# RWKV-7 scan and a cosine-gated expert layer on one core: the ways of x^T in chunks 1 to 3, and three instead of four conversion steps between two steps of chunk 1

## The chip, the cores and the metric

The kernel runs on one core of a Trainium2 chip. The metric is the device time of one execution in microseconds (us), lower being better. It is compared by medians of several executions. Engines are named as in the profile: PE is TensorE (matmuls), PEld its weight loads, DVE is VectorE, ACT is ScalarE, POOL is GpSimd, and SP is SyncE, whose queue issues nearly all DMAs of the stretch that this document is about.

## The reference

```python
# attention: r, k, v, w, a, b are (4, 8, 768, 40)
for t in range(S):
    y[:, :, t] = np.einsum('bhd,bhde->bhe', rt, state)
    Sa = np.einsum('bhde,bhe->bhd', state, at)
    state_decay = state * wt[:, :, None, :] - np.einsum('bhd,bhe->bhde', Sa, bt)
    state = state_decay + np.einsum('bhd,bhe->bhde', vt, kt)
# bridge: x is (3072, 320), one row per batch and position
h = x @ w_in            # 320 -> 2048
g = h * np.cos(h)
out = g @ w_out         # 2048 -> 320
```

The inputs of the attention are float32. `w_in` and `w_out` come as float64 and are used as float32, so the kernel reads their 64-bit words and makes float32 of them itself.

## The kernel before

The 768 positions go in 24 chunks of 32. Each chunk turns the recurrence into small matrix products and a triangular solve; only the state goes from one chunk to the next. Two chunks make a group of 256 tokens for the expert layer. The whole program's order is written out by hand: every engine works its instructions in the order in which the Python code records them, and waits where an operand isn't ready.

**One chunk.** `main(c)` gives five segments: `t` (`ch_t`, transposes the state `qz` into `s`), `q` (`ch_q`), `x` (`ch_x`, right sides; copied to `x0` by ACT and DVE), `s` (`ch_s`, the solve by the inverse `rt`; its result is copied and masked into `sm`), and `z` (`ch_z`, products `dps` that give the new state `qz` and the output `yt`). `p2(c + 1)` gives three segments that prepare the next chunk: `v`, `k` and `g` (`p2_g`, the products `gram`, masked into `ag` and `vvm`). Every four chunks need an inverse, made on DVE by `by_blocks` or `inverse`. For chunks 0 to 7 its lower half is made by TensorE instead, one chunk at a time: `pair_first` (`F1`, `F2`, ...) and `pair_second` (`S1`, `S2`, ...), whose sum goes into `rt` on DVE (L567). `p1(c)` gives `pw`, `pa`, `pb`, `pn`, which prepare decays and inverse for two chunks from 4 on; they hold the reciprocals L395.

**The way of x^T.** In `ch_z` DVE writes `yt` by four additions (L762), which alternate with four for the state (L755); POOL scales the state in four products (L756) and then multiplies `yt` by the decay (L767). Two segments later `tokens` stores `yt` to a buffer `xd` in HBM (L776), and one segment later `back` loads it as `xT` (L786, L788). Both go on SP, and the load waits for the store.

**Expert layer.** `pieces` is a list of short works: `first_a` and `first_b` make `ph = xT . w_in` for a quarter of the 2048 columns, followed by rounding, cosine and product (`turns`, L830 to L840, giving `gT`); `second` makes `po = gT . w_out`. In the lists of segments an `M` stands where the next piece goes. A group's pieces may run from the chunk after its second one.

**The weights' conversion.** The weights are cut into 20 blocks of 128x512. For each, `rounded` gives `fetch` (SP, L237), `taken` (DVE L245 and L246, ACT L249 and L251), `mantissa` (DVE L255, ACT L258) and `product` (DVE L261, then POOL L264 for the sign). `w_steps` lists them mixed: product of n, fetch of n + 3, mantissa of n + 1, taken of n + 2. `step(seg, of_inv, of_w)` records a segment, then what was put off with `later` and is due, then `of_inv` steps of the inverse and `of_w` of `w_steps`. The pair comes from `fill`: (1, 4) in chunk 1, (0, 2) in chunk 2, (2, 3) in chunk 3. `F` and `S` segments before chunk 3 pass (0, 0). `later(n, ...)` counts segments, so a segment more or less moves what is put off. What is left of `w_steps` is recorded before `pn4`.

**The scan of w.** `ws_scan` makes running products of the decays of four chunks at once, nine operations on DVE (L170 and L175). `scanned(q)` does it, puts off the store to HBM (`ws_store`, L180) by two segments and the fetch of the next four chunks (`ws_fetch`, L161) by twelve. `scanned(2)` stands in chunk 3.

**Idle fills.** `busy(n)` and `kept_busy(n)` record n matmuls on zeros that nothing reads. `busy` follows each segment of chunk 1, and those of chunk 2 until the first piece is done; `FILL` maps (chunk, place in the list) to a count for `kept_busy`.

**Buffers.** Most products go to the PSUM pool `at`, which has two buffers: a segment that takes one waits until the last but one user has been read. `ph` and `po` have pools of two buffers each.

Of the kernel before, what the change touches and what calls it, by code (L numbers as in the profile page):

```python
# [20 lines left out]
def kernel(  # L21
# [43 lines left out]
    nc = tc.nc  # L65
# [97 lines left out]
            bass.AP(w.tensor, w.offset + q * n, [[S * D, B * H], [C * D, 4], [1, C * D]]),  # L163
        )

    def ws_scan(q):
        n = 1
        while n < C:
            to = ws[:, 2 * n - 1 :: 2 * n]
            nc.vector.tensor_tensor(to, to, ws[:, n - 1 :: 2 * n], ALU.mult)  # L170
            n *= 2
        n = C // 4
        while n:
            to = ws[:, 3 * n - 1 :: 2 * n]
            nc.vector.tensor_tensor(to, to, ws[:, 2 * n - 1 : C - 1 : 2 * n], ALU.mult)  # L175
            n //= 2

    def ws_store(q):
        wd[q] = dram.tile([B, H, 4, C, D], F32, tag="wd", name="wd")
# [546 lines left out]
    def ch_z(c):  # L726
        ps = [at("dps") for _ in range(2)]
        sm = G["sm"]

        wide = c > 3  # L730
        for bb in range(0 if wide else B):
            for e in range(2):
                mm(
                    ps[bb // 2][full[e], bb % 2, : 4 * N72], idle[blk[bb], :DP],
                    pick(idle[blk[bb]], 0, (0, 4), (1, N72)), True,
                )
        for s, n in ((0, kn_b[c % 2]), (1, bn_b[c % 7])):
            for j in range(4):
                o = C - C * (j // 2)
                for bb in range(B):  # L740
                    for e in range(2):
                        first = wide and not s
                        mm(
                            ps[bb // 2][(full if first else half)[e], bb % 2, j * N72 : (j + 1) * N72],
                            n[blk[bb], 2 * j + e, : DP if first else D],
                            sm[e][blk[bb], j, :] if s else vvm[c % 2][blk[bb], 2 * j + e, o : o + N72],
                            first and j == 0,
                        )
        wx, wc = G["wx", c], G["wc", c]
        yt = sb1.tile([P, 4, B, C], F32, tag="yt", name="yt")  # L750
        for bb in range(B):
            dp = ps[bb // 2][:, bb % 2]
            if c < NCH - 1:
                z = pick(qz[:, bb], C, (DP, 2), (NZ, 2), (1, D))
                nc.vector.tensor_tensor(z, pick(dp, 0, (2 * N72 + C, 2), (N72, 2), (1, D)), z, ALU.add)  # L755
                nc.gpsimd.tensor_tensor(  # L756
                    z, z,
                    wc.rearrange("p (f m b) -> p f m b", f=2, m=2)[:, :, :, bb]
                    .unsqueeze(3).to_broadcast([P, 2, 2, D]),
                    ALU.mult,  # L760
                )
            nc.vector.tensor_tensor(  # L762
                yt.rearrange("p (f m) b t -> p f m b t", f=2)[:, :, :, bb],
                pick(dp, D, (2 * N72 - D, 2), (N72, 2), (1, C)),
                pick(qz[:, bb], 0, (NZ - C, 2), (NZ, 2), (1, C)), ALU.add,
            )
        nc.gpsimd.tensor_tensor(  # L767
            yt.rearrange("p j b t -> p (j b) t"), yt.rearrange("p j b t -> p (j b) t"), wx, ALU.mult
        )
        later(2, lambda: tokens(c, yt))  # L770
# [133 lines left out]

        return [first_w, both_a, lambda: p1_b(c), lambda: p1_n(c)]

    def scanned(q):

        ws_scan(q)
        later(2, lambda: ws_store(q))  # L910
        if q + 1 < NCH // 4:
            later(12, lambda: ws_fetch(q + 1))
# [17 lines left out]
    with tc.manual_schedule():  # L930
# [115 lines left out]
        firsts = [lambda n=n: pair_first(0, n, n > 2) for n in range(4)]  # L1046
        seconds = [lambda n=n: pair_second(0, n, n > 2) for n in range(4)]
        (F1, F2, F3), (S1, S2, S3) = firsts[1:], seconds[1:]
        FILL = {(1, 6): 6, (1, 9): 14, (2, 0): 6, (2, 3): 6, (2, 5): 4, (2, 11): 29, (3, 3): 13, (3, 4): 20}
        for c in range(NCH):  # L1050
            t, q, x, s, z = main(c)
            v, k, g = p2(c + 1) if c + 1 < NCH else [lambda: None] * 3
# [2 lines left out]
            if c == 0:  # L1055
                segs = []
            elif c == 1:
                segs, fill = [t, F1, v, q, k, S1, x, g, s, z], (1, 4)
            elif c == 2:
                for n, m, name in ((11, 5, "a"), (14, 4, "b")):  # L1060
                    later(n, lambda m=m, name=name: load(m, name))
                segs, fill = [t, F2, v, q, S2, k, M, x, M, F3, g, M, s, S3, M, z, M, M], (0, 2)
            elif c == 3:
                pw4, pa4, pb4, pn4 = p1(4)
                pw, pa, pb, pn = p1(6)
                segs = [
                    t, pw4, M, q, pa4, M, x, lambda: scanned(2), M, s, pw, M, pb4, pa, M, pn4, M, z, M,
                    pb, v, pn, k, M, g,
                ]
                for n, m, name in ((1, 5, "b"),):  # L1070
                    later(n, lambda m=m, name=name: load(m, name))
                fill = (2, 3)
            elif c == 4:
                pw, pa, *p8 = p1(8)
                firsts = [lambda n=n: pair_first(4, n) for n in range(4)]
                seconds = [lambda n=n: pair_second(4, n) for n in range(4)]
                F4, F5, F6, F7 = firsts
                S4, S5, S6, S7 = seconds
                segs = [
                    t, v, M, q, M, k, x, M, F4, M, S4, F5, M, s, F6, M, pw, F7, M, z, M, g, M, pa, S5, lambda: scanned(3),  # L1080
                ]
                fill = (2, 0)
            elif c == 5:
                pw, pa = p1(10)[:2]
                pb, pn = p8
                segs = [t, M, pb, q, M, pn, k, M, x, M, s, S6, M, z, M, S7, M, pw, v, M, g, pa, M]
            elif c % 4 == 0 and q0 < NCH:
                pb, pn = p1(q0)[2:]
                segs = [t, v, M, q, M, k, x, M, g, M, s, pb, M, z, M, pn, M, M]
                if q0 + 4 < NCH:  # L1090
                    segs.insert(-1, lambda: scanned(c // 4 + 2))
            elif c % 4 == 1 and q0 < NCH:
                pw, pa = p1(q0 + 2)[:2]
                segs = [t, M, pw, q, M, x, k, M, s, v, M, z, M, pa, M, g, M, M]
            elif c % 4 == 2 and q0 < NCH:
                pb, pn = p1(q0 + 2)[2:]
                segs = [t, M, pb, q, M, pn, v, M, x, M, s, k, M, g, M, z, M, M]
            elif c % 4 == 3 and q0 + 4 < NCH:
                pw, pa = p1(q0 + 4)[:2]
                segs = [t, M, pw, q, M, x, k, M, s, v, M, z, M, pa, M, g, M, M]  # L1100
            else:
                segs = [t, v, M, q, M, x, k, M, g, M, s, M, M, z, M, M]
# [10 lines left out]
            for i, seg in enumerate(segs):  # L1113
# [7 lines left out]
                    w_steps.pop(0)()  # L1121
                if seg is not M:
                    G["kind"] = "q" if seg is q and c > 3 else "other"
                    step(seg, *((0, 0) if c < 3 and seg in (*firsts, *seconds) else fill), small=seg in (q, x, g, s, z, pn, pn4, *firsts, *seconds))
                    if seg not in (*firsts, *seconds) and (c < 2 or c == 2 and not done):
                        busy({s: 6, q: 5, v: 4, k: 4, z: 4}.get(seg, 3))
                else:
# [45 lines left out]
```

## Time and profile before

| what | us |
| --- | --- |
| median of 3 runs | 802.15 |
| the runs | 800.43, 803.71, 802.15 |
| profiled execution | 800.58 |
| its span, first to last instruction | 798.9 |
| PE busy | 745.9 (93%) |
| PEld busy | 571.0 (71%) |
| DVE busy | 486.7 (61%) |
| ACT busy | 383.4 (48%) |
| POOL busy | 199.9 (25%) |
| last `yt` addition (L762) of chunks 0, 1, 2, 3, start | 61.97, 92.28, 126.08, 161.45 |
| product L767 of these chunks, start | 62.55, 94.11, 126.66, 162.09 |
| store `xd` issued | 64.30, 95.59, 127.95, 165.10 |
| load `xT` issued | 69.42, 97.87, 130.23, 170.00 |
| first operation of the scan in chunk 3, last one's end | 145.93, 149.87 |

The table's busy times are sums over the span. The idle fills count as busy time of PE, and so does the time in which matmuls queue in it. What one stretch is limited by is read from that stretch alone: from the busy time of each engine in a window cut at the chunks' borders, from the timeline, where an instruction carries the idle time before it and what ended that in brackets, and from the chain of waits.

### The profile page before, as it was taken

What the parts mean: (1) busy time and instruction counts of PE and PEld (TensorE: products, weight loads), DVE (VectorE), ACT (ScalarE), POOL (GpSimd) and SP (SyncE); (2) the same over time, 40 slices, a digit from 0 to 9 for tenths busy, and PEclk for the clock granted to TensorE, in tenths of its full rate; (3) what the DMA queues carried; (4) which work ended last, traced back from release to release, by engine and by line L of the source; (5) the groups of instructions that cost most, each with busy time, mean ns of one, the idle gap of its engine ahead of it and who ended that gap; (6) DMA issues with size and microseconds to landing.
All of it is one profiled execution on the core that took longest, in us unless ns stands there. A gap on an engine that the chain in (4) does not pass through costs nothing.

```text
span 798.9 us, 39602 instructions
## 1 busy us (share of the span) xinstructions
PE 745.9 (93%) x17812; PEld 571.0 (71%) x17812; DVE 486.7 (61%) x1025; ACT 383.4 (48%) x723; POOL 199.9 (25%) x354
## 2 busy tenths in 40 slices
PE   4768798999999999999999999999999999999997
PEld 4535576777766777777777787777787777777775
DVE  8768858864734896554895645994346863323331
ACT  1336567564435436545535635534545445354352
POOL 5326635230321330330330230332031122201000
PEclk9888899999999999999999999999999999999999
DMA  8575563343353314334214324223220222001000
GB/s 112 150 187 140 146 152 88 60 124 64 59 122 64 67 36 65 72 99 70 60 38 66 93 43 73 46 49 68 43 46 21 46 46 55 19 18 32 20 17 16
DMA packets 183304, 55.79 MB, mean 70 GB/s; under 512 B 157152, under 2 KB 178656, under 8 KB 183136
## 3 DMA queue, kind: packets, MB, share of 16 engines
q1 hardware_dynamic: 177440, 52.11, 30.6%
q8 instruction: 140, 2.29, 1.2%
q10 hardware_dynamic: 5440, 0.82, 0.8%
q0 software_dynamic: 256, 0.33, 0.3%
q14 instruction: 28, 0.23, 0.1%
HBM read 42.07 MB, written 11.14 MB: 67 GB/s over the span
## 4 chain that ended last, share of the span: by engine, by line
PE 65%; DVE 14%; DMA 5%; ACT 5%; issue 4%; POOL 3%; SPq 2%; DVEq 0%; ACTq 0%; POOLq 0%
PE ph L101 22%; PE po L101 20%; PE x0ps L101 3%; PE dps L101 3%; PE gram L101 3%; DVE rw L395 3%; PE vT L330 2%; PE sps L101 2%; PE qps L101 2%; PE nps L101 2%; DVE inv_tmp L494 2%; DVE inv L498 2%; DVE mant L245 1%; SPq L152 1%; PE kT L330 1%
## 5 line engine op out<-in xcount | busy, mean ns | idle before, releaser
L101 PE MATMUL po<-w_out_sb,gT 128*128 128x320 f32 x768 | 223.5, 439 | 0.1
L101 PE MATMUL ph<-xT,w_in_sb 128*128 128x256 f32 x768 | 185.7, 386 | 0.1
L101 PEld LDWEIGHTS po<-w_out_sb,gT 128*128 128x128 f32 x768 | 140.2, 190 | 54.6 <-issue 2.3
L101 PEld LDWEIGHTS ph<-xT,w_in_sb 128*128 128x128 f32 x768 | 139.3, 190 | 29.7 <-issue 12.4
L830 ACT ACTIVATE turns<-ph,rnd 128x512 f32<-128x512 f32 x96 | 64.1, 685 | 156.3 <-PE ph L101 155.9
L832 DVE SCALAR_TENSOR_TENSOR turns<-turns,ph 128x512 f32<-128x512 f32 x96 | 64.0, 683 | 109.4 <-ACT turns L830 109.2
L840 DVE TENSOR_TENSOR gT<-ph,turns 128x512 f32<-128x512 f32 x96 | 65.8, 686 | 38.4 <-ACT turns L837 38.4
L756 POOL TENSOR_TENSOR qz<-qz,wc 128x160 f32<-128x160 f32 x92 | 41.9, 475 | 168.5 <-DVE qz L755 167.9
L837 ACT ACTIVATE turns<-turns,half_pi 128x512 f32<-128x512 f32 x96 | 69.3, 722 | 3.1
L836 ACT ACTIVATE turns<-turns 128x512 f32<-128x512 f32 x96 | 60.1, 626 | 19.0 <-DVE turns L832 19.0
L101 PE MATMUL ph<-xT,w_in_tail 64*128 64x256 f32 (+1 forms) x512 | 54.6, 394 | 1.6 <-issue 1.6
L498 DVE TENSOR_TENSOR inv<-inv,inv_tmp 128x31 f32<-128x31 f32 (+15 forms) x124 | 51.2, 413 | 4.3
L755 DVE TENSOR_TENSOR qz<-dps,qz 128x160 f32<-128x160 f32 x92 | 28.9, 314 | 37.6 <-PE dps L101 37.3
L586 POOL COPY vp<-nat_v 128x320 f32<-128x320 f32 x24 | 11.7, 487 | 159.9 <-DMA nat_v<-in_v_dram 139.6
L494 DVE TENSOR_TENSOR inv_tmp<-u,inv 128x31 f32<-128x31 f32 (+15 forms) x124 | 48.5, 391 | 2.3
L395 DVE RECIPROCAL rw<-nat_w 128x320 f32<-128x320 f32 x20 | 42.8, 2142 | 0.1
L101 PEld LDWEIGHTS ph<-xT,w_in_tail 64*128 64x128 f32 (+1 forms) x512 | 32.2, 160 | 10.8 <-issue 7.3
L767 POOL TENSOR_TENSOR yt<-yt,wb 128x512 f32<-128x512 f32 x24 | 31.6, 1318 | 22.1 <-DVE yt L762 22.1
L659 ACT COPY s<-sT 104x416 f32<-104x416 f32 x46 | 20.8, 503 | 33.1 <-PE sT L655 33.1
L719 DVE TENSOR_TENSOR sm<-sps,su 128x128 f32<-128x128 f32 x48 | 11.7, 285 | 33.1 <-ACT sm L714 30.3
L396 POOL TENSOR_TENSOR bn<-nat_b,rw 128x320 f32<-128x320 f32 x22 | 19.9, 905 | 44.3 <-DVE rw L395 44.2
L671 ACT COPY qz<-qps 40x512 f32<-40x512 f32 x46 | 26.6, 579 | 6.8 <-PE qps L101 6.4
(136 smaller groups left out, 1100.3 us busy)
## 6 DMA issues: line engine op xcount, KB each, us to landing
words<-in_moe_w_in_dram SPq DMA_DIRECT2D x8, 512.0 KB
xd<-yt SPq DMA_DIRECT2D x48, 80.0 KB
out_dram<-ot SPq DMA_DIRECT2D x24, 160.0 KB
nat_k<-in_k_dram SPq DMA_DIRECT2D x92, 40.0 KB
nat_v<-in_v_dram SPq DMA_DIRECT2D x92, 40.0 KB
nat_r<-in_r_dram SPq DMA_DIRECT2D x92, 40.0 KB
nat_a<-in_a_dram SPq DMA_DIRECT2D x84, 40.0 KB
ws<-in_w_dram SPq DMA_DIRECT2D x5, 640.0 KB
```

The costliest lines, as they stand in the source:

```text
L101: nc.tensor.matmul(o, lhsT=lhsT, rhs=rhs, start=start, stop=stop, skip_group_check=True)
L395: nc.vector.reciprocal(rw, wn)
L494: nc.vector.tensor_tensor(tmp, u[:, j : j + 1, :j].to_broadcast([P, C - j, j]), x[:, j:, j : j + 1].to_broadcast([P, C - j, j]), ALU.mult,)
L498: nc.vector.tensor_tensor(x[:, j:, :j], x[:, j:, :j], tmp, ALU.subtract)
L755: nc.vector.tensor_tensor(z, pick(dp, 0, (2 * N72 + C, 2), (N72, 2), (1, D)), z, ALU.add)
L756: nc.gpsimd.tensor_tensor(z, z, wc.rearrange("p (f m b) -> p f m b", f=2, m=2)[:, :, :, bb] .unsqueeze(3).to_broadcast([P, 2, 2, D]), ALU. ...
L767: nc.gpsimd.tensor_tensor(yt.rearrange("p j b t -> p (j b) t"), yt.rearrange("p j b t -> p (j b) t"), wx, ALU.mult)
L830: nc.scalar.activation(n, u, ACTF.Identity, bias=rnd, scale=1.0)
L832: nc.vector.scalar_tensor_tensor(n, n, -ROUND, u, ALU.add, ALU.subtract)
L836: nc.scalar.activation(n, n, ACTF.Abs)
L837: nc.scalar.activation(n, n, ACTF.Sin, bias=half_pi, scale=-2.0 * math.pi)
L840: nc.vector.tensor_tensor(gT[:, 2 * e : 2 * e + 2].rearrange("p f t -> p (f t)"), us[e], ns[e], ALU.mult)
```

## The change

Five things are edited.

- In chunk 1, `fill` is (1, 3) instead of (1, 4).
- In `ch_z` the last product of `yt` goes to DVE instead of POOL in chunks 1 and 3.
- `ws_scan` can do a part of its nine operations, `scanned` takes the bounds, and puts off store and fetch with the last part alone. `scanned(2)` moves from chunk 3 to chunk 2, in three parts of three operations, each with no steps of conversion.
- In chunk 2 the first `M` goes from before `x` to behind it, and `S3` from before `z` to behind the piece that follows `z`. There are still six `M`. The key of the 29 fills goes from (2, 11) to (2, 13), the same piece. In chunk 3 the last segment `g` goes to chunk 4, behind `t`, and a piece follows it there that stood behind `v`. Chunks 3 and 4 have as many `M` as before.
- In chunk 5 `S6` and `S7` go further behind.

```diff
@@ -163,17 +163,17 @@
             bass.AP(w.tensor, w.offset + q * n, [[S * D, B * H], [C * D, 4], [1, C * D]]),
         )
 
-    def ws_scan(q):
-        n = 1
+    def ws_scan(lo=0, hi=9):
+        work, n = [], 1
         while n < C:
-            to = ws[:, 2 * n - 1 :: 2 * n]
-            nc.vector.tensor_tensor(to, to, ws[:, n - 1 :: 2 * n], ALU.mult)
+            work.append((ws[:, 2 * n - 1 :: 2 * n], ws[:, n - 1 :: 2 * n]))
             n *= 2
         n = C // 4
         while n:
-            to = ws[:, 3 * n - 1 :: 2 * n]
-            nc.vector.tensor_tensor(to, to, ws[:, 2 * n - 1 : C - 1 : 2 * n], ALU.mult)
+            work.append((ws[:, 3 * n - 1 :: 2 * n], ws[:, 2 * n - 1 : C - 1 : 2 * n]))
             n //= 2
+        for to, by in work[lo:hi]:
+            nc.vector.tensor_tensor(to, to, by, ALU.mult)
 
     def ws_store(q):
         wd[q] = dram.tile([B, H, 4, C, D], F32, tag="wd", name="wd")
@@ -764,7 +764,7 @@
                 pick(dp, D, (2 * N72 - D, 2), (N72, 2), (1, C)),
                 pick(qz[:, bb], 0, (NZ - C, 2), (NZ, 2), (1, C)), ALU.add,
             )
-        nc.gpsimd.tensor_tensor(
+        (nc.vector if c in (1, 3) else nc.gpsimd).tensor_tensor(
             yt.rearrange("p j b t -> p (j b) t"), yt.rearrange("p j b t -> p (j b) t"), wx, ALU.mult
         )
         later(2, lambda: tokens(c, yt))
@@ -904,9 +904,11 @@
 
         return [first_w, both_a, lambda: p1_b(c), lambda: p1_n(c)]
 
-    def scanned(q):
-
-        ws_scan(q)
+    def scanned(q, lo=0, hi=9):
+
+        ws_scan(lo, hi)
+        if hi < 9:
+            return
         later(2, lambda: ws_store(q))
         if q + 1 < NCH // 4:
             later(12, lambda: ws_fetch(q + 1))
@@ -1046,7 +1048,8 @@
         firsts = [lambda n=n: pair_first(0, n, n > 2) for n in range(4)]
         seconds = [lambda n=n: pair_second(0, n, n > 2) for n in range(4)]
         (F1, F2, F3), (S1, S2, S3) = firsts[1:], seconds[1:]
-        FILL = {(1, 6): 6, (1, 9): 14, (2, 0): 6, (2, 3): 6, (2, 5): 4, (2, 11): 29, (3, 3): 13, (3, 4): 20}
+        FILL = {(1, 6): 6, (1, 9): 14, (2, 0): 6, (2, 3): 6, (2, 5): 4, (2, 13): 29, (3, 3): 13, (3, 4): 20}
+        scan = []
         for c in range(NCH):
             t, q, x, s, z = main(c)
             v, k, g = p2(c + 1) if c + 1 < NCH else [lambda: None] * 3
@@ -1055,18 +1058,20 @@
             if c == 0:
                 segs = []
             elif c == 1:
-                segs, fill = [t, F1, v, q, k, S1, x, g, s, z], (1, 4)
+                segs, fill = [t, F1, v, q, k, S1, x, g, s, z], (1, 3)
             elif c == 2:
                 for n, m, name in ((11, 5, "a"), (14, 4, "b")):
                     later(n, lambda m=m, name=name: load(m, name))
-                segs, fill = [t, F2, v, q, S2, k, M, x, M, F3, g, M, s, S3, M, z, M, M], (0, 2)
+                scan = [lambda n=n: scanned(2, n, n + 3) for n in (0, 3, 6)]
+                segs, fill = [t, F2, v, q, S2, k, x, M, scan[0], M, F3, g, scan[1], M, s, scan[2], M, z, M, S3, M], (0, 2)
             elif c == 3:
                 pw4, pa4, pb4, pn4 = p1(4)
                 pw, pa, pb, pn = p1(6)
                 segs = [
-                    t, pw4, M, q, pa4, M, x, lambda: scanned(2), M, s, pw, M, pb4, pa, M, pn4, M, z, M,
-                    pb, v, pn, k, M, g,
+                    t, pw4, M, q, pa4, M, x, M, s, pw, M, pb4, pa, M, pn4, M, z, M,
+                    pb, v, pn, k, M,
                 ]
+                g4 = g
                 for n, m, name in ((1, 5, "b"),):
                     later(n, lambda m=m, name=name: load(m, name))
                 fill = (2, 3)
@@ -1077,13 +1082,13 @@
                 F4, F5, F6, F7 = firsts
                 S4, S5, S6, S7 = seconds
                 segs = [
-                    t, v, M, q, M, k, x, M, F4, M, S4, F5, M, s, F6, M, pw, F7, M, z, M, g, M, pa, S5, lambda: scanned(3),
+                    t, g4, M, v, q, M, k, x, M, F4, M, S4, F5, M, s, F6, M, pw, F7, M, z, M, g, M, pa, S5, lambda: scanned(3),
                 ]
                 fill = (2, 0)
             elif c == 5:
                 pw, pa = p1(10)[:2]
                 pb, pn = p8
-                segs = [t, M, pb, q, M, pn, k, M, x, M, s, S6, M, z, M, S7, M, pw, v, M, g, pa, M]
+                segs = [t, M, pb, q, M, pn, k, M, x, M, s, M, z, M, S6, M, pw, S7, v, M, g, pa, M]
             elif c % 4 == 0 and q0 < NCH:
                 pb, pn = p1(q0)[2:]
                 segs = [t, v, M, q, M, k, x, M, g, M, s, pb, M, z, M, pn, M, M]
@@ -1121,7 +1126,7 @@
                     w_steps.pop(0)()
                 if seg is not M:
                     G["kind"] = "q" if seg is q and c > 3 else "other"
-                    step(seg, *((0, 0) if c < 3 and seg in (*firsts, *seconds) else fill), small=seg in (q, x, g, s, z, pn, pn4, *firsts, *seconds))
+                    step(seg, *((0, 0) if c < 3 and seg in (*firsts, *seconds, *scan) else fill), small=seg in (q, x, g, s, z, pn, pn4, *firsts, *seconds))
                     if seg not in (*firsts, *seconds) and (c < 2 or c == 2 and not done):
                         busy({s: 6, q: 5, v: 4, k: 4, z: 4}.get(seg, 3))
                 else:
```

## The prediction

> **What bounds the kernel now.** I read the windows first, cut at the chunks' borders: chunk 1 is 62.2 to 92.6 us, chunk 2 runs to 126.3, chunk 3 to 160, and 145.4 is the end of the VectorE copy that chunk 3's solve (`ch_s`) waits for. The columns are the stretch, its length, then the busy time and count of PE, PEld, DVE, ACT and POOL, then the granted clock, the DMA share and GB/s.
>
> ```profile
> 62.20:92.60 30.40, 23.47 (x720) 14.66 (x719) 26.96 (x48) 20.24 (x36) 18.24 (x18) 0.85 0.54 135
> 92.60:126.30 33.70, 31.00 (x913) 23.62 (x911) 23.69 (x47) 24.49 (x44) 15.30 (x19) 1.00 0.61 151
> 126.30:145.40 19.10, 17.81 (x293) 13.94 (x292) 17.00 (x24) 12.12 (x21) 10.44 (x14) 1.00 0.25 55
> 145.40:160.00 14.60, 14.01 (x383) 11.20 (x384) 11.95 (x21) 7.12 (x16) 2.58 (x6) 1.00 0.47 73
> ```
>
> Chunk 1 is VectorE's: 26.96 of 30.40 us busy, while TensorE waits for 7 us and has idle fills in its 23.47. Chunk 2 is TensorE's (31.00 of 33.70), and VectorE has 10.0 us left over. The first 19 us of chunk 3 belong to both. From 145.4 on TensorE runs dense. Second, the chain of waits, which shows what a piece of the weights' conversion costs in chunk 1 (start, us, what):
>
> ```profile
> 71.92 0.68 DVE w_out_sb L261
> 72.60 0.60 DVE mant L255
> 73.20 1.31 DVE mant L245
> 74.58 0.19 issue
> 74.77 0.68 DVE w_out_sb L261
> ```
>
> From product to product is 2.85 us. The four operations alone are 0.42 + 0.42 + 0.68 + 0.68 = 2.20 us. The rest is L245 at 1.31 instead of 0.42, each time beside GpSimd's sign product L264. Third, the timeline, where TensorE pays for it:
>
> ```profile
> 88.43 0.32 PE L101 MATMUL dps<-idle 32*64 32x288 bf16 x4 [3.30 <-DVE sm L719]
> ...
> 91.81 2.35 POOL L756 TENSOR_TENSOR qz<-qz,wc 128x160 f32<-128x160 f32 x4
> ...
> 94.11 1.46 POOL L767 TENSOR_TENSOR yt<-yt,wb 128x512 f32<-128x512 f32 x1
> ...
> 94.21 0.39 PE L655 MATMUL sT<-ident,qz 104*104 104x104 f32 x2 [0.21 <-POOL qz L756]
> ```
>
> Before `dps` (`ch_z` of chunk 1) TensorE stands for 3.30 us behind VectorE's mask of `sm`. Chunk 2 opens when GpSimd has scaled the state.
>
> **Chunk 1, three steps instead of four.** Eight segments pass `fill`, so eight conversion steps, that is two pieces of four steps, leave the chunk. VectorE loses 2 x 2.85 = 5.7 us. TensorE can give back only its waits: 3.30 for `sm`, 0.56 for `vvm`, and 0.84 before `sps` (for `x`), together 4.7; the rest of its time is work, fills and two gaps (1.0 and 1.54 us) for which the profile shows no releaser. I take 4.5. One sign product that kept GpSimd until 91.85, though VectorE's first `qz` ended at 91.08, is no longer just ahead: 0.5 more. So -5.0, with ends -3.3 (only the long wait goes) and -6.2 (all of VectorE's 5.7 and the 0.5).
>
> **x^T of chunk 1 on VectorE.** L767 took 1.46 us on GpSimd, behind four `qz` scalings. On VectorE the nearest row is the 128x512 product L840 at 0.68 us; beside GpSimd a product L261 took 1.76 (at 94.36). x^T lands some 2.3 us earlier. But the first `ph` started at 102.44, straight behind the idle fill that began at 101.58, while x^T's last load was issued at 98.30. I cost the gain at nothing. The 0.7 to 1.8 us on VectorE lie in chunk 2's 10.0 us.
>
> **Chunk 2.** The first expert piece goes behind `x`, so `x` gets three idle matmuls, because nothing is done yet: 0.8 us (three took 0.82 at 75.17). The scan's nine operations took 2.21 + 1.82 us at L170 and L175 in chunk 3, about 3.9 with their spacing; as three groups they fall into VectorE's gaps (2.86 before `x`, 1.28 before `vvm`, 1.16 before `sm`, 1.12 before `turns`). The last two groups, 2.1 us, and pieces that come 0.9 later meet 2.9 us of gaps in the second half, so I let `ch_z` come 0.8 late there. Against it, `S3` no longer stands ahead of `dps`, which waited 0.72 us for its sum `rt` (L567), and 0.6 of matmuls go behind it; it then delays the next state transposes, which are hidden by chunk 3's own wait. The gaps may cover everything, or nothing of the last two groups. Sum +0.4, ends -1.4 and +1.9.
>
> The scan's store (640 KB) and the next fetch go with it onto SP. They leave the place where SP stood 1.7 us for the store just ahead of chunk 3's `xd`. In chunk 2 they go between two fetches of weights; the second rival is about that.
>
> **Chunk 3, up to the copy of `x`.** Here the two pieces come back. VectorE carries, from the last `gT` of chunk 2 to the `turns` ahead of `x`, five instead of three products and four instead of two pairs of L245 and L246. That is 2 x 2.85 = 5.7, plus 0.25 for the moved `rt`, less a gap of 0.85 before a product, at 138.72, which the pieces fill: 5.1. With L245 slowed only once in a while (one of two was in this stretch), it is some 4.6, which I take. Ends: 2.3 (2 x 2.20 less all 2.1 us that VectorE idles here) and 5.9 (nothing covered). All of it shows, since behind this copy stands `sps`:
>
> ```profile
> 144.95 0.46 DVE L697 COPY x<-x0ps 128x288 f32<-128x288 f32 x1 [1.14 <-ACT x L696]
> ...
> 145.47 0.86 PE L101 MATMUL sps<-x,rt 32*32 32x72 f32 x62 [0.18 <-DVE x L697]
> ```
>
> TensorE came there only 0.5 us early, so it will now stand some 4 us, and everything queued behind `sps` on it with it.
>
> **What the scan leaves in chunk 3.** 3.9 us of VectorE go, but TensorE was busy for 14.01 of 14.60 us there; only 0.35 us of waiting for `sm` before `aps` ends: -0.4 (ends 0 and -0.6).
>
> **Chunks 4 and 5.** The gram products of chunk 5's `p2` are now behind the state transposes and ahead of an expert piece, which needs no `at` buffer. That covers a wait of 0.62 us (`vT` behind `vvm`, at 171.20): -0.6, ends 0 and -1.1. The price is that x^T of chunk 3 must be there some 1.5 us earlier. It can: its last product moves from GpSimd (1.27 us, behind four scalings) to VectorE, and SP's 1.7 us go. `S6` behind `ch_z` takes 0.33 us ahead of `dps` (at 225.54) away: -0.3, ends 0 and -0.6. `S7` moves among dense work: nothing; were its sum late, chunk 7 would wait, far off.
>
> **The clock.** The long wait of chunk 1 is followed by slow rows (stretch, length, PE busy, clock, DMA share, GB/s):
>
> ```profile
> 85.00:90.00 5.00, 1.70 (x112) 0.86 0.75 226
> 90.00:95.00 5.00, 4.51 (x67) 0.79 0.49 123
> ```
>
> At 0.79, 4.51 us of work lose 0.95. A wait of 4 us in chunk 3 buys the same, while chunk 1's goes; chunk 1 has idle fills to soak it up, chunk 3 behind `sps` doesn't. I take +0.6, ends 0 and +0.95. The Trainium skill's page "TensorE: Matmul & The Clock Gate" (section "What's actually happening") speaks against the change: one idle window of about 3.4 us puts the array on half rate until a busy window has passed. By that rule, an estimate, 3.4 us at half rate would cost 1.7 instead of 0.6, and the sum would come 1.1 higher. The row shows a milder loss, 0.79 over 5 us, so the row decides.
>
> **Sum.** -5.0 + 0.4 + 4.6 - 0.4 - 0.6 - 0.3 + 0.6 = -0.7 us. The profiled execution took 800.58 (its span 798.9 and 1.7 around it), and would take 799.9. The median of the three runs, 802.15, lies 1.57 above it: 801.4. So the two pieces are carried from where VectorE holds TensorE up to another such place, and what is left is small. Over or under 0.5% (4.0 us) is about what a measurement of this kernel tells from no change, the three runs being 3.3 us apart.
>
> **Rivals.** *Faster.* The pieces really vanish in chunk 3: VectorE's idle 2.1 us take them without slowdowns (+2.3), and chunk 1, no longer stalled, gets its clock back. Its mean of 0.85 over 23.47 us of TensorE work is 3.5 us lost; half of it back is -1.8. Then -5.0 + 0.4 + 2.3 - 1.3 - 1.8 = -5.4, so 796.8. For it: TensorE has 12.44 of 13.80 us busy early in chunk 1, so the clock is what is left to gain. Against: VectorE is dense from 126.9 to 143.8.
>
> *Slower.* The last fetches of weights come late. On SP the last two now stand behind x^T of chunk 2, which waits for its store (SP waited 8.3 us in four such places), and behind four loads of `nat_b`; 640 KB of the scan go out shortly before. Piece 18 would be issued some 9 us behind the chunk's start and land 2.7 us later (the 2.71 of the row at 104.81), which is about when VectorE wants it. 640 KB at the 122 GB/s of 120 to 130 us are 5.4 us. If they fall into that wait, VectorE stands, and behind it `x` and `sps`: 801.4 + 5.4 = 806.8. It decides once the fetch lands over 1 us after the product of piece 16. For it: VectorE did stand 0.76 us for `words` at 107.64. Against: that stretch moves only 52 to 55 GB/s.
>
> *Half of the gain only.* If TensorE's gaps without releaser grow with the denser chunk 1, only 3.3 is had there: 803.1.
>
> **Chances.** Forecast 0.31, half gain 0.09 (both within 0.5%), faster 0.30, slower 0.30. All lower ends together give -6.2 - 1.4 + 2.3 - 0.6 - 1.1 - 0.6 = -7.6, all upper ones -3.3 + 1.9 + 5.9 + 0.95 = +5.5; with the slower rival on top 808 is passed. I take 796 to 807.5; the forecast's own range is 798.5 to 804.5.
>
> **What would show it.** Right: the wait of `dps` for `sm` in chunk 1 falls from 3.30 us to under 0.5; chunk 2's first `sT` starts near 88; its length stays 33 to 35; `sps` of chunk 3 waits 3 to 5 us for VectorE's `x`, near 145; the wait of 0.62 at `vT` is gone. Wrong: `sps` of chunk 3 starts before 142 (faster), or L245 stands for DMA `words` in chunk 3 (slower).

## The result: half a per cent slower, lost in chunk 2

The changed kernel takes 805.78 us (median of 14 runs), the kernel before 802.5 (14 runs beside them). The ratio is 1.005, with a 95% interval of 1.0035 to 1.0065: slower, by 4.0 us on 802.5. The forecast was 801.4. The profiled execution of the changed kernel has a span of 804.2 us, against 798.9.

The windows of the changed kernel, cut as those of before were (stretch, length, then busy time and count of PE, PEld, DVE, ACT, POOL, then clock, DMA share, GB/s). Chunk 1 starts at 60.4, chunk 2 at 87.9, chunk 3 at 127.4, and 152.4 is the end of its copy of `x`:

```profile
60.40:87.90 27.50, 22.81 (x717) 13.96 (x718) 20.10 (x39) 16.26 (x30) 16.07 (x18) 0.81 0.53 126
87.90:127.40 39.50, 33.40 (x918) 25.46 (x916) 29.58 (x57) 24.02 (x44) 12.62 (x16) 0.91 0.51 131
127.40:152.40 25.00, 22.07 (x297) 16.45 (x291) 22.93 (x33) 16.42 (x28) 14.23 (x16) 0.80 0.38 98
152.40:167.00 14.60, 13.99 (x383) 11.50 (x384) 8.78 (x12) 8.08 (x17) 2.61 (x7) 1.00 0.59 115
```

Chunk 1 is shorter. Chunk 2 has 39.5 us instead of 33.7, and neither TensorE nor VectorE fills it. For the rest of this text a chunk is measured from the first addition of the state (L755, `qz<-dps`) of one `ch_z` to that of the next, and chunk 3 is cut at VectorE's copy of `x` (L697). All in us:

| stretch | before | after | difference | forecast |
| --- | --- | --- | --- | --- |
| up to chunk 0's state | 60.45 | 58.61 | -1.84 | 0 |
| chunk 1 | 30.31 | 27.52 | -2.79 | -5.0 |
| chunk 2 | 33.79 | 39.52 | +5.73 | +0.4 |
| chunk 3 up to `x` | 20.40 | 26.25 | +5.85 | +4.6 |
| chunk 3 behind `x` | 14.97 | 14.80 | -0.17 | -0.4 |
| chunk 4 | 40.67 | 39.19 | -1.48 | -0.6 |
| chunk 5 | 26.54 | 25.56 | -0.98 | -0.3 |

The forecast's +0.6 for the clock is in no row. Behind chunk 5 another 0.98 us is added; with it the column gives the 5.3 us between the spans. The first row lies ahead of every edit and shows how far one execution strays from another.

In chunk 2 VectorE stands. Its timeline in the changed kernel, and one line of TensorE's (start, us, instruction, in brackets the idle time before it and what ended that):

```profile
99.71 0.68 DVE L255 SCALAR_TENSOR_TENSOR mant<-words,mant 128x512 f32<-128x512 uint32 x1
105.49 0.43 DVE L245 TENSOR_SCALAR mant<-words 128x512 int32<-128x512 int32 x1 [5.10 <-DMA words<-in_moe_w_in_dram]
...
106.17 0.68 DVE L261 TENSOR_TENSOR w_in_sb<-mant,expo 128x512 f32<-128x512 f32 x1
106.78 2.54 DVE L176 TENSOR_TENSOR ws<-ws 128x640 f32<-128x640 f32 x3
109.23 1.28 DVE L832 SCALAR_TENSOR_TENSOR turns<-turns,ph 128x512 f32<-128x512 f32 x2
...
112.20 3.75 PE L101 MATMUL ph<-xT,w_in_sb 128*128 128x256 f32 x8 [3.69 <-DVE gT L840]
```

From 100.39 to 105.49 VectorE waits for the `words` of block 12, the first tail of `w_in`. Behind that wait stand the first part of the scan and the `turns` of the first expert piece, and TensorE waits 3.69 us for the product `gT` that follows. SP shows why the block is late. First SP's issues in the kernel before, then those of the changed one:

```profile
84.74 7.84 SPq L237 DMA_DIRECT2D words<-in_moe_w_in_dram  x6
93.30 0.81 SPq L237 DMA_DIRECT2D words<-in_moe_w_out_dram  x2
95.59 0.72 SPq L776 DMA_DIRECT2D xd<-yt  x2
97.87 0.39 SPq L786 DMA_DIRECT2D xT<-xd  x1
```

```profile
89.96 0.76 SPq L776 DMA_DIRECT2D xd<-yt  x2
94.70 0.39 SPq L786 DMA_DIRECT2D xT<-xd  x1
95.13 1.12 SPq L788 DMA_DIRECT2D xT<-xd  x2
96.34 3.37 SPq L152 DMA_DIRECT2D nat_k<-in_k_dram  x4
99.81 3.27 SPq L237 DMA_DIRECT2D words<-in_moe_w_in_dram  x4
```

Before, the four fetches of block 12 are the last of the six at 84.74, ahead of the store `xd`. With three steps the same step of the list is recorded in a later segment, and so behind `xd`, behind the load of x^T that waits for it until 94.70, and behind `nat_k`. The chain of waits of the changed kernel runs through this place, and again through a fetch in chunk 3 (start, us, what; SPq is SP's queue):

```profile
97.41 1.80 SPq L152
...
99.81 0.48 SPq L237
...
101.61 3.76 DMA words<-in_moe_w_in_dram
...
107.62 1.34 DVE ws L176
...
137.16 5.81 DMA words<-in_moe_w_out_dram
```

The step of 1.34 us at `ws` is a second finding; in chunk 3 of the kernel before, one operation of this scan took at most 0.82 us. It comes back below.

### The profile page after: what moved, and what is told of

Same layout as the page of the kernel before. It is cut to its first block, busy times and chain, and to the rows that moved or that the text cites. A ratio compares the mean times of both kernels' runs of the same rounds, so it can differ in the third digit from the quotient of the medians.

```text
span 804.2 us, 39610 instructions
## 1 busy us (share of the span) xinstructions
PE 752.7 (94%) x17815; PEld 574.8 (71%) x17815; DVE 489.7 (61%) x1027; ACT 383.4 (48%) x723; POOL 198.3 (25%) x352
## 4 chain that ended last, share of the span: by engine, by line
PE 65%; DVE 17%; DMA 5%; ACT 4%; issue 3%; SPq 3%; POOL 2%; DVEq 0%; ACTq 0%; POOLq 0%
PE ph L101 22%; PE po L101 20%; PE x0ps L101 4%; PE dps L101 3%; PE gram L101 3%; DVE rw L395 2%; PE sps L101 2%; PE vT L330 2%; DVE inv_tmp L494 2%; SPq L152 2%; DVE inv L498 2%; PE nps L101 2%; PE qps L101 2%; DMA xd<-yt 1%; DVE turns L832 1%
## 5 line engine op out<-in xcount | busy, mean ns | idle before, releaser
L101 PE MATMUL po<-w_out_sb,gT 128*128 128x320 f32 x768 | 227.4, 445 | 0.1
L101 PEld LDWEIGHTS po<-w_out_sb,gT 128*128 128x128 f32 x768 | 142.1, 192 | 55.8 <-issue 4.5
L840 DVE TENSOR_TENSOR gT<-ph,turns 128x512 f32<-128x512 f32 x96 | 65.8, 687 | 38.6 <-ACT turns L837 38.6
L755 DVE TENSOR_TENSOR qz<-dps,qz 128x160 f32<-128x160 f32 x92 | 29.1, 316 | 37.1 <-PE dps L101 37.1
L659 ACT COPY s<-sT 104x416 f32<-104x416 f32 x46 | 20.8, 503 | 35.2 <-PE sT L655 35.2
L767 POOL TENSOR_TENSOR yt<-yt,wb 128x512 f32<-128x512 f32 x22 | 28.9, 1313 | 22.1 <-DVE yt L762 22.1
L642 ACT COPY vvm<-gram 128x256 f32<-128x256 f32 x24 | 8.8, 369 | 44.0 <-DVE ag L637 43.6
```

The source lines that it names most:

```text
L101: nc.tensor.matmul(o, lhsT=lhsT, rhs=rhs, start=start, stop=stop, skip_group_check=True)
L767: (nc.vector if c in (1, 3) else nc.gpsimd).tensor_tensor(yt.rearrange("p j b t -> p (j b) t"), yt.rearrange("p j b t -> p (j b) t"), wx, ...
L840: nc.vector.tensor_tensor(gT[:, 2 * e : 2 * e + 2].rearrange("p f t -> p (f t)"), us[e], ns[e], ALU.mult)
```

## The experiments

Each run is given as its ratio to the kernel before, measured beside it on the same chip, with the 95% interval. 0.1% is 0.8 us. Lengths and waits are from the run's one profile. The expectations in us reckon with 802.15 for the kernel before. Beside the scan alone, chunks 4 and 5 alone and the first two runs with all fetches earlier it took 799.38, so there the ratio times 802.15 is what is held against them.

**The edits one at a time.** The three steps alone, on the kernel before:

```diff
-                segs, fill = [t, F1, v, q, k, S1, x, g, s, z], (1, 4)
+                segs, fill = [t, F1, v, q, k, S1, x, g, s, z], (1, 3)
```

> The kernel before with (1, 3) in chunk 1 and nothing else. Theory of the late fetch: VectorE waits 3 to 6 us at L245 in chunk 2 and the scan still lies in chunk 3, so 804 to 809. Rival (the other edits cost the time): 800 to 803, with chunk 1 some 3 us shorter and chunk 3 some 4 longer.

1.0057 (1.0025 to 1.0089), the theory's range. By the ratio the three steps alone are as slow as the whole change, but they lose it elsewhere. VectorE waits 2.74 us for words in chunk 2 (3 to 6 were expected), which without the scan has 34.7 us, only 0.9 more than before. It waits 3.55 in chunk 3, whose part up to `x` takes 27.2 us. This profile is of the slowest of its runs (811.51).

The reverse, on the changed kernel:

```diff
-                segs, fill = [t, F1, v, q, k, S1, x, g, s, z], (1, 3)
+                segs, fill = [t, F1, v, q, k, S1, x, g, s, z], (1, 4)
```

> The changed kernel with (1, 4) in chunk 1, the rest of the change kept. Theory: the loss is the late fetch of the tail block of w_in (four loads), which three steps push behind x^T's load and nat_k in SP's queue; VectorE then stood 5.10 us at L245 for it. With four steps that fetch stands ahead of chunk 1's xd again: the wait at L245 in chunk 2 is under 1 us, chunk 2 lasts 33 to 35 us from its predecessor's first qz to its own instead of 39.5, and the time is 798 to 802.5, at or under the kernel before. Rival (the moved scan, x^T on VectorE and the reordered pieces cost the time): it stays at 804 to 807.

1.0034 (1.0015 to 1.0054). The median, 803.72 us, lies just under the rival's range, and the ratio times 802.15, 804.9, inside it: the rest of the change costs something too. The theory's signs didn't come. Chunk 2 has 39.8 us, with a wait of 4.06 for words of `w_out`: block 12 is in time, but three loads of the next block are issued at 105.64, behind x^T's load and `nat_k`. So words come late in chunk 2 with four steps too, once the rest of the change is there.

The changed kernel with L767 on GpSimd in all chunks:

```diff
-        (nc.vector if c in (1, 3) else nc.gpsimd).tensor_tensor(
+        nc.gpsimd.tensor_tensor(
```

> The changed kernel with the last product of yt on GpSimd in all chunks. Theory of the late fetch: x^T isn't the gate, so the time stays within 1.5 us of the changed kernel's 805.8; the tail's fetch stands behind x^T's load, which waits for the store, so it comes 1 to 2 us later and the wait at L245 grows by as much, which gives 805.5 to 808. Rival (the product on VectorE costs its 0.92 us there twice): 804 to 805.

1.0048 (1.0029 to 1.0068), the changed kernel's own within the intervals. x^T's last product on VectorE shows no worth, as was forecast. The wait for words didn't grow by 1 to 2 us, as the theory had it; it is 4.36 instead of 5.10.

The scan in chunk 2 alone, on the kernel before (with `ws_scan` and `scanned` as changed):

```diff
-                segs, fill = [t, F2, v, q, S2, k, M, x, M, F3, g, M, s, S3, M, z, M, M], (0, 2)
+                segs, fill = [t, F2, v, q, S2, k, M, x, M, scan[0], F3, g, scan[1], M, s, scan[2], S3, M, z, M, M], (0, 2)
...
-                    t, pw4, M, q, pa4, M, x, lambda: scanned(2), M, s, pw, M, pb4, pa, M, pn4, M, z, M,
+                    t, pw4, M, q, pa4, M, x, M, s, pw, M, pb4, pa, M, pn4, M, z, M,
```

> The kernel before with one edit: the scan in three parts in chunk 2 instead of chunk 3. Theory (late words): the scan lies in VectorE's gaps and nothing is behind it that words would not hold; 801 to 803. Rival (full VectorE): its about 4 us and its store delay the mask of sm and the state's turn in chunk 2, chunk 2 grows by 2 to 4 us and chunk 3 gives back 0.4; 803.5 to 806.

1.0017 (0.9996 to 1.0038), that is 803.5, the lower end of the rival's range, and not distinguishable from the kernel before. Chunk 2 does grow, to 37.1 us, but chunks 4 and 5 are 2.0 us shorter together. Here the scan's store and the fetch that waits for it no longer stand on SP ahead of chunk 3's `xd`, and the load of this x^T is issued 5.8 us after chunk 3's first addition of the state instead of 10.1. The same holds throughout: in the ten profiles with the scan in chunk 2 that load comes after 5.0 to 5.8 us and chunk 4 has 38.6 to 39.7 us; in the other ten it comes after 6.2 to 11.9, and chunk 4 has 39.0 to 45.2.

The order of chunk 2 alone:

```diff
-                segs, fill = [t, F2, v, q, S2, k, M, x, M, F3, g, M, s, S3, M, z, M, M], (0, 2)
+                segs, fill = [t, F2, v, q, S2, k, x, M, M, F3, g, M, s, M, z, M, S3, M], (0, 2)
```

> The kernel before with the order of chunk 2 alone: first expert piece behind x, S3 behind the piece that follows z; no scan there. Forecast of the prediction: about 0 (0.8 us of idle matmuls and 0.9 of later pieces, less 0.72 of waiting for rt), ratio 0.998 to 1.002. Rival: S3, which takes a buffer that the state products hold until VectorE's additions, stalls TensorE by some 2.4 us behind z; 1.003 to 1.006.

1.0034 (1.001 to 1.0058): the rival's range, but its mechanism has to be tried alone. VectorE waits 2.12 us for words in chunk 2 here, against 0.17 with the scan alone, so it is the order that goes with the wait at four steps. `S3` alone:

> The kernel before with S3 alone moved behind the piece that follows z. Theory (S3 waits there for a buffer that dps holds until VectorE's additions, and TensorE with it): all of the 0.34% of the order, 1.002 to 1.005. Rival: the cost came from the first piece, 0.9 us later and three idle matmuls more; 0.998 to 1.001.

0.9993 (0.9972 to 1.0014). `S3`'s wait is there, 1.50 us in this profile and 2.42 in the changed kernel's (`below` is `S3`'s product):

```profile
126.74 0.72 PE L101 MATMUL below<-rt,bn 32*32 32x16 f32 x64 [2.42 <-DVE yt L762]
```

but no cost shows: the wait is not the order's price. That leaves the first piece behind `x`; in the profile of the whole order chunk 2 has 33.5 us, not more than before, so where the 0.34% go isn't shown.

The edits of chunks 4 and 5 alone, on the kernel before:

```diff
-                    pb, v, pn, k, M, g,
+                    pb, v, pn, k, M,
...
-                    t, v, M, q, M, k, x, M, F4, M, S4, F5, M, s, F6, M, pw, F7, M, z, M, g, M, pa, S5, lambda: scanned(3),
+                    t, g4, M, v, q, M, k, x, M, F4, M, S4, F5, M, s, F6, M, pw, F7, M, z, M, g, M, pa, S5, lambda: scanned(3),
...
-                segs = [t, M, pb, q, M, pn, k, M, x, M, s, S6, M, z, M, S7, M, pw, v, M, g, pa, M]
+                segs = [t, M, pb, q, M, pn, k, M, x, M, s, M, z, M, S6, M, pw, S7, v, M, g, pa, M]
```

> The kernel before with the edits of chunks 4 and 5 alone (the gram of chunk 3 behind t of chunk 4, S6 and S7 later in chunk 5). The profile of the changed kernel has 1.5 and 1.0 us less in these chunks. Theory: these are gains of their own, 799 to 801. Rival: they only follow from a later start of chunk 4, with x^T and pieces already there; 801.5 to 803.

0.9983 (0.9959 to 1.0007), that is 800.8: in the theory's range, and the lowest ratio of all runs, though its interval holds 1. In its profile chunk 5 is 0.9 us shorter, but chunk 4 is not (40.8 us).

**Fetching earlier.** First block 12 alone, in the changed kernel, two steps earlier:

```diff
+        early = w_steps.index(w_work[12][0])
+        w_steps.insert(early - 2, w_steps.pop(early))
```

> The changed kernel with the fetch of the tail block two conversion steps earlier: on SP it stands behind x^T's load and ahead of nat_k's four loads. Theory of the late fetch: it is issued some 3.4 us earlier, the wait of 5.10 us falls to 1 to 2 us, and the time by 2 to 4 us, to 801.5 to 804. Rival (the wait is covered by the 29 fills and by TensorE's other work, the loss is VectorE's work in chunk 3): within 1 us of 805.8.

1.0037 (1.0016 to 1.0057). The wait in chunk 2 falls from 5.10 to 1.29 us and chunk 2 to 36.2, but chunk 3 now waits 2.76 for a later block. Against 1.005 the gain is within the intervals, so the time decides nothing here.

Then all blocks from 10 on:

```diff
-            if nxt < len(w_work):
+            if nxt < len(w_work) and n < 7:
                 w_steps.append(w_work[nxt][0])
             if n + 1 < len(w_work):
                 w_steps.append(w_work[n + 1][2])
+            if 7 <= n + 1 and n + 4 < len(w_work):
+                w_steps.append(w_work[n + 4][0])
```

> The changed kernel with each fetch from block 10 on recorded three steps earlier, straight behind the mantissa that frees its buffer. Theory (late words): what the change loses in chunks 2 and 3 is VectorE standing for words that SP issues late; now no wait of L245 for words above 1 us is left in chunks 2 and 3, and the time falls by 3 to 5 us, to 799 to 802.5. Rival (full VectorE): the scan and the later expert pieces fill VectorE in chunk 2, and the wait for words only stood where another wait would; then 803 to 806.

1.0013 (0.9988 to 1.0037), 3.0 us less than the changed kernel by the ratios. The fall and the waits are the theory's (one is left, 0.67 us in chunk 3), while the 803.2 us that the ratio makes are at the lower edge of the rival's range: something besides the words is left. Chunk 2 has 36.6 us, and chunk 3 up to `x` 24.9. The same edit on the kernel before:

> The kernel before with the same earlier fetches as in the run of the changed kernel. Theory (late words): it stood only 0.76 us for words, so it moves little, 800.5 to 802.5. Rival: the time SP spends waiting for a buffer ahead of xd delays x^T, 803 to 806.

1.0035 (1.0012 to 1.0059), that is 805.0. The rival held: there the fetch stands ahead of `xd` either way, and SP now stands longer for the buffers (SP's issues in this run):

```profile
82.90 11.47 SPq L237 DMA_DIRECT2D words<-in_moe_w_in_dram  x6
96.08 1.50 SPq L237 DMA_DIRECT2D words<-in_moe_w_out_dram  x2
97.63 0.77 SPq L776 DMA_DIRECT2D xd<-yt  x2
```

Six fetches spread over 11.47 us instead of 7.84, and chunk 1 takes 32.4 us instead of 30.3. An earlier fetch is no gain in itself.

The three steps and the earlier fetches, nothing else:

> The kernel before with three steps in chunk 1 and with the earlier fetches; nothing else of the change. Alone the three steps took it to 1.0057, the earlier fetches to 1.0035. Theory (late words): what three steps cost is words that come late, since a step less per segment puts the block's fetch behind x^T on SP; with the fetches earlier the ratio is 0.997 to 1.001, and chunk 1 is some 4 us shorter, chunk 3 some 4 longer. Rival: the two costs add up, as the earlier fetches keep SP ahead of xd; 1.006 to 1.01.

1.0023 (1.0002 to 1.0045), just outside the theory's range, but the costs don't add up as the rival had it. It is 0.34% under the three steps alone, which is about what the two intervals leave open. With the edits of chunks 4 and 5 as well:

> The run before it plus the edits of chunks 4 and 5, the candidate to beat both kernels. Theory: 0.994 to 0.999. Rival (costs add up): 1.004 to 1.008.

0.999 (0.9963 to 1.0016), the upper end of the theory's range; not distinguishable from the kernel before.

The changed kernel with the order of before in chunk 2 (the scan's parts stay), with late fetches and with early ones:

```diff
-                segs, fill = [t, F2, v, q, S2, k, x, M, scan[0], M, F3, g, scan[1], M, s, scan[2], M, z, M, S3, M], (0, 2)
+                segs, fill = [t, F2, v, q, S2, k, M, x, M, scan[0], F3, g, scan[1], M, s, scan[2], S3, M, z, M, M], (0, 2)
```

> The changed kernel (1.005) with the order of before in chunk 2, fetches as late as in the changed kernel. Theory (account adds up): 1.000 to 1.003. Rival (late words hold chunk 2 whatever the order): 1.004 to 1.006, with a wait for words of 4 us or more in chunk 2.

1.0062 (1.004 to 1.0084): the rival's side, just above its range, with a wait of 3.79 us. Beside late words, with the scan in chunk 2, the order shows no effect.

> The changed kernel with the earlier fetches and with chunk 2's pieces and S3 in the order of before (the scan's three parts stay in chunk 2). Account so far, each from its own run: three steps with late words 0.57%, order of chunk 2 0.34, scan 0.17 alone but -0.43 beside three steps, chunks 4 and 5 -0.17. Theory (the account adds up): the changed kernel with earlier fetches had 1.0013, less 0.34: 0.996 to 1.000, the best so far. Rival: with the words in time, the order of chunk 2 no longer decides anything; 1.000 to 1.003.

1.0001 (0.9979 to 1.0022), where the two ranges meet; 0.61% under the run before it. So three pairs of kernels with three steps, late and early fetches, point one way: 1.0057 and 1.0023, 1.005 and 1.0013, 1.0062 and 1.0001. The last two differences are clear of the intervals, the first is not. But in the last two pairs a second thing changes with the fetches: what the scan stands beside. The changed kernel (VectorE and GpSimd, start, us):

```profile
115.27 0.69 DVE L261 TENSOR_TENSOR w_in_tail<-mant,expo 128x512 f32<-128x512 f32 x1
...
115.87 1.83 DVE L176 TENSOR_TENSOR ws<-ws 128x80 f32<-128x80 f32 x3
...
116.10 1.16 POOL L264 TENSOR_TENSOR w_in_tail<-w_in_tail,sign 128x512 f32<-128x512 f32 x1 [7.30 <-ACT expo L249]
```

and the same part of the scan in the changed kernel with all fetches earlier:

```profile
111.69 0.58 DVE L176 TENSOR_TENSOR ws<-ws 128x80 f32<-128x80 f32 x3
...
112.20 0.69 DVE L261 TENSOR_TENSOR w_in_tail<-mant,expo 128x512 f32<-128x512 f32 x1
...
113.03 1.47 POOL L264 TENSOR_TENSOR w_in_tail<-w_in_tail,sign 128x512 f32<-128x512 f32 x1 [3.42 <-DVE w_in_tail L261]
```

In the changed kernel each part of the scan stands straight behind a product L261, whose sign product GpSimd starts beside it. The three operations take 1.83 us instead of 0.58, and all nine 2.54 + 1.83 + 2.51 = 6.88 instead of 1.69 + 0.58 + 1.58 = 3.85 (4.03 in chunk 3 before). There GpSimd stood idle from 144.88 on, and then had only small copies and fills, 0.86 us in all:

```profile
148.23 0.21 POOL L380 COPY wc<-wb 128x16 f32<-128x16 f32 x1 [3.35 <-ACT wb L378]
```

Only the pair without the scan prices the words alone, at 0.34%, and that isn't clear of the noise.

The scan back in chunk 3, on the changed kernel with the earlier fetches:

```diff
-                segs, fill = [t, F2, v, q, S2, k, x, M, scan[0], M, F3, g, scan[1], M, s, scan[2], M, z, M, S3, M], (0, 2)
+                segs, fill = [t, F2, v, q, S2, k, x, M, M, F3, g, M, s, M, z, M, S3, M], (0, 2)
...
-                    t, pw4, M, q, pa4, M, x, M, s, pw, M, pb4, pa, M, pn4, M, z, M,
+                    t, pw4, M, q, pa4, M, x, lambda: scanned(2), M, s, pw, M, pb4, pa, M, pn4, M, z, M,
```

> The changed kernel with the earlier fetches (1.0013 when the scan is in chunk 2) and with the scan back in chunk 3. If the scan is what still makes chunk 2 longer (36.6 us there against 33.8), chunk 2 falls by 2 to 3 us, chunk 3 gains 0.4 to 1 and the ratio is 0.995 to 0.999. If S3's place and the later first piece make it, chunk 2 stays above 35.5 and the ratio at 1.000 to 1.003.

1.0056 (1.0028 to 1.0084). Neither range, and 0.43% over the scan in chunk 2. The two pieces in chunk 3 aren't the reason: the run at 0.999 has them too, with the scan in chunk 3 and the same fetches. It differs in the order of chunk 2 and in x^T's last product, which showed no worth. So the order costs where the scan stands in chunk 3 (0.34% alone, 0.66% between these two runs), and shows nothing where it stands in chunk 2 (1.005 and 1.0062, 1.0013 and 1.0001). The profile doesn't say why. Its span, 798.9 us, belongs to the lowest of the runs (800.68 to 811.49), so it is no picture of the median.

**Another queue.** The fetches of blocks 12 to 19 on GpSimd's queue, at their places in the list:

```diff
-                nc.sync.dma_start(
+                (nc.gpsimd if m > 11 else nc.sync).dma_start(
```

> The changed kernel with the fetches of blocks 12 to 19 issued on GpSimd's queue, at the same places in the order of the conversion, so that they stand behind nothing of x^T, k, v, r, a and b on SP. Theory (what makes the words late is SP's queue): the wait of L245 for words in chunk 2 falls from 5.1 us to under 1.5, the ratio from 1.005 to 0.998 to 1.002, as the earlier fetches on SP gave. Rival (the fetch is simply recorded too few steps ahead of its use, on whatever queue): the wait stays above 2.5 us, 1.003 to 1.006. Against both: GpSimd's own issuing takes its time from the state's scaling and from VectorE; 1.006 or more.

1.006 (1.0033 to 1.0086). Chunk 2 has no wait for words any more, so SP's queue had made that one; but chunk 2 still takes 38.4 us, with a scan of 6.88, and in chunk 3 the waits return (VectorE, then GpSimd):

```profile
133.61 0.43 DVE L245 TENSOR_SCALAR mant<-words 128x512 int32<-128x512 int32 x1 [2.09 <-DMA words<-in_moe_w_in_dram]
144.40 0.43 DVE L245 TENSOR_SCALAR mant<-words 128x512 int32<-128x512 int32 x1 [3.25 <-DMA words<-in_moe_w_out_dram]
...
137.94 1.10 POOL L396 TENSOR_TENSOR bn<-nat_b,rw 128x320 f32<-128x320 f32 x1
139.00 1.60 POOL L264 TENSOR_TENSOR w_in_sb<-w_in_sb,sign 128x512 f32<-128x512 f32 x1
140.55 1.13 POOL L237 DMA_DIRECT2D words<-in_moe_w_out_dram  x2
```

On GpSimd the fetch stands behind `bn` and the sign product instead of behind x^T. So both halves are true: SP's queue made the words late in chunk 2, and so short a lead is lost on the other queue too. The ratio also fits the third expectation, that issuing costs GpSimd time of its own; no run prices that alone.

> The changed kernel with the old order of chunk 2 (1.0062) and the same fetches on GpSimd's queue. Theory (SP's queue): 0.997 to 1.002. Rival: 1.004 to 1.007.

1.0066 (1.0039 to 1.0093): the same.

> The kernel before with the edits of chunks 4 and 5 (0.9983) and the fetches of blocks 12 to 19 on GpSimd's queue. With four steps the words came on time on SP, so the theory sees 0 from it but the 0.76 us before L245 and a freer SP: 0.995 to 0.999, the candidate to beat both. Rival (GpSimd issues at a cost): 1.000 to 1.004.

1.0003 (0.9976 to 1.003), the rival's range. Here VectorE waits 3.91 us for words at 101.55, ahead of chunk 2's `x`, and chunk 2 still has 34.6 us: the waits for words there add up to 5.4 us, and without a scan there is room for them. No version was shown to beat the kernel before.

**What chunk 2 has room for.** The profiles of the 18 runs and of both kernels fall into three classes. The second column adds the waits for words in chunk 2 and the scan's time there:

| chunk 2 | wait + scan, us | length, us |
| --- | --- | --- |
| no scan (before and 9 runs) | 0 to 5.4 | 33.1 to 36.3 |
| scan, waits of at most 1.3 us (6 runs) | 3.9 to 8.2 | 36.2 to 38.6, one 43.0 |
| scan, waits from 3.8 us (after and 3 runs) | 9.8 to 12.0 | 39.0 to 39.8 |

Against the 33.8 us of before, waits alone (2.1 to 5.4 us, three runs) cost at most 0.9 us, the scan with little waiting 2.4 to 4.8, the one of 43.0 aside, and both together 5.2 to 6.0. The one of 43.0 had its clock at 0.77 for the first 22.75 us, in a run whose median ratio is 1.0001: one profile can lie several us beside its kernel's median.

## Why the prediction was wrong

The step that failed is chunk 2, put at "+0.4, ends -1.4 and +1.9". It said that the scan's "about 3.9" us "as three groups ... fall into VectorE's gaps", of which it counted 10.0 us. Two terms were wrong. The scan's size: 6.88 us, since each part was put where GpSimd's sign product runs beside it; the 3.9 came from a place where GpSimd had none. And a term that was missing: the words of block 12, 5.10 us. Wait and scan together are 12.0 us for those gaps, and x^T's product took another 0.92. Chunk 2 grew by 5.73, and that alone turns the sum: with 5.7 in place of 0.4 the forecast's -0.7 becomes +4.6 us, near the 4.0 measured. That it comes so near is luck in part: the other rows and the clock miss by +2.2, +1.3, +0.2, -0.9, -0.7 and -0.6, which nearly cancel. (The step's terms as listed, 0.8 + 0.8 - 0.72 - 0.6, make 0.3 rather than 0.4, which is nothing beside this.)

The slower rival had the mechanism, "the last fetches of weights come late", but the wrong place: it looked at the last two blocks, in chunk 3, where waits of 0.76 and 0.17 us came. It named x^T's wait on SP and `nat_b`'s loads; the same reading of SP's order one chunk earlier, for the blocks that move past chunk 1's `xd`, would have found block 12. Its price, 806.8 us, lies near the measured time by another sum. The prediction had counted what three steps take from VectorE, but, beyond the last two blocks, not where they put the fetches on SP.

The other steps:

- **Chunk 1, -5.0.** Mis-sized. The wait of `dps` for `sm` is gone and chunk 2's first `sT` starts near 88, as foretold:

```profile
84.42 0.33 PE L101 MATMUL dps<-idle 32*64 32x288 bf16 x8
...
87.64 0.38 PE L101 MATMUL busy<-idle 128*128 128x512 bf16 x1 [0.80 <-issue]
...
88.35 0.88 PE L655 MATMUL sT<-ident,qz 104*104 104x104 f32 x8
```

  But 1.84 us of that were there before the chunk began, and the chunk is only 2.79 us shorter; in the eleven runs with three steps and the changed kernel it has 25.1 to 28.2 us, on the mean 26.7, which is 3.6 less than before. The gaps of TensorE without a releaser were 1.0 and 1.54 us and are now 1.49, 1.66 and 0.80. That is the rival called half gain, of which the gaps' growth is seen but not its cause.
- **Chunk 3 up to `x`, +4.6.** Right. All profiles with four steps have 20.4 to 20.8 us there, the five with three steps and earlier fetches 24.9 to 25.3, that is +4.5 to +4.9. The changed kernel's 5.85 hold 0.93 of waits for words besides. What was to show it was wrong: `sps` doesn't stand 3 to 5 us; it follows `x` at once, and TensorE stood earlier, by 2.52 us before `x0ps`.

```profile
144.86 1.26 PE L101 MATMUL x0ps<-vvm,ag 32*32 32x72 f32 x64 [2.52 <-ACT qz L671]
151.92 0.31 PE L101 MATMUL sps<-x,rt 32*32 32x72 f32 x2 [0.18 <-ACT x L696]
```

- **x^T on VectorE, 0.** Right, 1.0048 without it.
- **Chunks 4 and 5, -0.9 together.** The wait at `vT` is gone. Alone these edits gave -0.17%, 1.4 us, whose interval holds both 0 and the forecast. The changed kernel's -1.48 in chunk 4 goes with the scan's move rather than with them: chunk 4 has 39.4 us with the scan alone and 40.8 with these edits alone.
- **The clock, +0.6.** Not seen: it doesn't set this stretch. The changed kernel and its twin with L767 on GpSimd have 0.80 and 0.94 in chunk 3 up to `x`, and 26.25 and 26.26 us:

```profile
125.65:151.90 26.25, 22.42 (x353) 16.98 (x353) 24.18 (x40) 17.64 (x31) 15.08 (x19) 0.80 0.40 105
```

```profile
125.75:152.01 26.26, 19.37 (x354) 15.23 (x353) 24.56 (x40) 17.64 (x31) 15.08 (x19) 0.94 0.40 105
```

VectorE's 24 us of work are nearer the bound there than the clock.

What stays open: how the loss in the changed kernel divides between late words and the slowed scan, and why the new order of chunk 2 costs where the scan stands in chunk 3 (`S3` alone shows no cost) and not where it stands in chunk 2.

## What to carry to other kernels

When steps are thinned out in a list that mixes computing with fetching, read what moves on the queue that issues the fetches, and past which waiting transfer, before counting what the computing engine saves. Fill an engine's gaps once only: a wait and a moved work may be meant for the same gap. And price a moved operation beside its new neighbours, not where it stood.

## What the hardware showed unexpectedly

A VectorE product with two operands in SBUF isn't slowed in proportion by a GpSimd product beside it, it stops: three operations of 0.58 us took 1.83, and the difference, 1.25, is about the one sign product of 1.16 us. In the other two parts the differences are 0.85 and 0.93, beside sign products of 1.67 and 1.16 us; the one of 1.67 started while an operation of the scan was running, and was itself the slower for it. The Trainium skill, page "SBUF — State Buffer", section "Who interferes with whom", says that these two share a read port under an exclusive lock and that the later one blocks until the earlier has ended; the rows agree with it.
